# A new written-out order of instructions for block-sparse attention followed by a gated projection

## The chip, the cores and the metric

One core of one Trainium2 chip. The metric is device time in microseconds, the median of several executions. The profiled execution is one more, with its own time.

## The reference

Inputs q, k and v have 4 batches, 8 heads, 768 rows and 64 columns; `w_in` is 512 x 2048, `w_out` 2048 x 512. Every query attends to its neighbours within 15 rows and to 24 block summaries, and the result runs through two products with a hard-swish between them:

```python
k_sum = k.reshape(B, H, nb, 32, D).max(axis=3)       # nb = 24
v_sum = v.reshape(B, H, nb, 32, D).mean(axis=3)
scores_l = where(|i - j| < 16, scale * q @ k.T, -1e9)
scores_s = scale * q @ k_sum.T + log(32)
a = softmax(concat([scores_l, scores_s]))
attn = a @ concat([v, v_sum])
...
h = x @ w_in                                          # x: 3072 x 512
g = h * clip(h + 3, 0, 6) / 6
out = g @ w_out
```

## The kernel before

Attention and the two products are worked off as one stream. The 3072 tokens make eight tiles `s` = 0 to 7 of 384 (two halves for each batch); queries go in groups of 64, each with a window of 96 keys and 24 summaries, 120 keys in all. Heads go in pairs `p` = 0 to 3.

The instructions of the five engines stand in the order that the string `ORDER` gives. Every operation registers itself under a key, with what it reads, writes and which PSUM or SBUF buffers it uses. `Plan.issue` goes through the string, takes the operation with that key, gives it the buffer that has been free longest, and issues it; waits follow from the data and the buffers. An engine executes its own operations in the order of the string, so a waiting one holds up all behind it on that engine. The letter behind a colon (`:A`, `:D`) picks ACT or DVE where either can do a copy.

The keys, as far as they matter here:

- `K`, `Q`, `V`, `I`, `O`, `H`: loads, all issued by POOL. `K00` to `K02`, `Q00`, `Q01` and `V00` to `V03` bring batch 0's keys, half of its queries and its values; `Q0w0` to `Q0w2` bring the rows of its other queries in three wide chunks (tile `qwide`, lines 318 to 326; chunk 0 is two transfers, of 16 and of 112 rows); `I0`, `I2`, `I4`, `I8`, `I12` bring columns of `w_in` from 0, 256, 512, 1024 and 1536 on (line 373); `K1*` and `Q1w*` are batch 1's keys and wide queries, `O*` is `w_out`.
- `k`, `q`: transposes of keys (line 391) and queries (420) on PE, with copies. `q3` and `q2` are those of the wide chunks (441); from `q4` on those of batch 1 (439).
- `sXYZ`: scores of batch X, pair or couple Y, half Z (489, 512), the exponential on ACT, the masking on DVE. In the first half of batch 0 a product with a mask stands ahead (`cover`, 481).
- `u`: sums of values (535, 553) and their copies; `h`: copies of values' halos.
- `v0p`: values of batch 0's first half, pair p (581), with the normalisation on DVE (598, 605), a transpose on PE (589) and a copy. `v411`, `v410` and so on: the same for two pairs of later halves (623, 636).
- `F{s}x{ft}`: a group of four products with `w_in` (666), `relu` on ACT (670), `gate` on DVE (671). For tile 0 the first five column groups are issued product by product, so that pair p's share can run as soon as it is there.
- `G{s}{ts}x...`: products with `w_out` (683) in four parts, a copy, and the store on SP.
- `w`: turning batch 1's and later keys on DVE (455) and what belongs to it.
- `_n`, `-n`, `~n`, `=n`: products of a tile of ones (line 771), whose result nobody reads. `_` and `-` are n products of 64 and of 128 columns, `~` n of 512, `=` one of n times 64.

PSUM has three banks `h`, one bank `o` and two double banks `S`. Loads go round eight semaphores, so that a load is issued once the one eight earlier has landed.

Of the kernel before, what the change touches and what calls it, by code (L numbers as in the profile page):

```python
# [37 lines left out]
F0x8.1 F0x8.2 F0x5.1 I0.0 F0x5.2 F0x11.0 F0x1.0 F0x11.1 F0x11.2 F0x1.1 F0x1.2 F0x1.3 F0x1.4 F0x1.5 v410.0 v410.1 F0x7.0 F0x7.1  # L38
F0x7.2 v410.2 F0x10.0 F0x10.1 I12.0 F0x13.0 F0x13.1 F0x15.0 F0x15.1 F0x13.2 F0x10.2 v411.3 v411.4:D v410.3 v410.4:A F0x15.2
F0x14.0 F0x14.1 F0x14.2 F0x9.0 F0x9.1 F0x9.2 F0x0.0 F0x0.1 F0x2.0 F0x2.1 K13.0 K10.0 c.12:A F0x0.2 K12.0 K11.0 w10.0 Q1w1.0  # L40
F1x14.0 F1x14.1 F1x14.2 F1x4.0 F1x4.1 F1x4.2 F1x2.0 F1x2.1 F1x2.2 w10.1:D F0x2.2 F0x2.3 F0x2.4 F0x12.0 F0x12.1 F0x12.2 F1x8.0
F1x8.1 F1x8.2 F1x1.0 F1x1.1 F1x1.2 F0x0.3 F0x0.4 F0x0.5 F0x2.5 F1x9.0 F1x9.1 F1x9.2 F1x5.0 F1x5.1 F1x5.2 F1x15.0 F1x15.1 w11.0
w11.2 F1x15.2 w11.3:D Q1w4.0 Q1w2.0 Q1w0.0 w10.2 w10.3:D q6.0 q6.1:A q7.0 q7.1:A F1x7.0 F1x7.1 w11.1:A F1x7.2 F1x12.0 F1x12.1
F1x12.2 O0.0 G02x0.0 Q1w5.0 Q1w3.0 q4.0 q4.1:A q5.0 q5.1:A F1x6.0 F1x6.1 F1x6.2 O1.0 G02x0.1 s100.0 s100.1 s100.3 F1x3.0 w12.0
F1x11.0 F1x11.1 w13.0 w13.2 F1x3.1 F1x11.2 w12.2 w12.1:D O2.0 G02x0.2 s101.0 s101.1 O3.0 F1x10.0 G02x0.3 G02x0.4:A w13.3:D
w13.1:A s101.3 F1x0.0 G00x0.0 G00x0.1 w12.3:D s100.2 s101.2 s100.4 V10.0 h100.0:D F1x10.1 h110.0:A F1x10.2 F1x3.2 s110.0 s110.1
s110.2 s101.4 s110.3 G00x0.2 G00x0.3 G00x0.4:A V12.0 u4.0 h130.0:D h120.0:A F1x0.1 u4.1:D u4.2:A u4.4:D u4.3:D u4.5:D G02x0.5
G01x0.0 G01x0.1 G01x0.2 s110.4 F1x0.2 h111.0:A v100.0 v100.1 v100.2 h121.0:A v101.0 v101.1 v101.2 G01x0.3 G01x0.4:A K20.0 K21.0
K22.0 K30.0 K23.0 w21.0 F1x13.0 F1x13.1 F1x13.2 v100.3 v100.4:A w20.0 w21.3 G12x0.0 w21.2:A v101.3 v101.4:A V22.0 H2.0 h101.0:A
w20.3 G12x0.1 G12x0.2 F2x2.0 F2x2.1 F2x11.0 F2x2.2 F2x11.1 F2x11.2 s111.0 w23.0 s111.3 F2x1.0 F2x1.1 F2x1.2 F2x3.0 F2x3.1 F2x3.2  # L50
F2x15.0 F2x15.1 F2x15.2 Q22.0 w23.3 G12x0.3 s111.1 G12x0.4:A F2x5.0 F2x5.1 h131.0:A F2x5.2 F2x6.0 G10x0.0 s111.2 w22.0 w22.3
s111.4 w23.4:A V20.0 H2.1:A K33.0 F2x13.0 F2x13.1 F2x13.2 G10x0.1 F2x6.1 F2x0.0 F2x0.1 F2x0.2 u5.0 u5.1:A u5.5:A F2x6.2 v110.0
v111.0 v111.1 v111.2 Q30.0 F2x4.0 F2x4.1 F2x4.2 Q21.0 Q23.0 Q20.0 w22.4:A F2x10.0 F2x10.1 F2x10.2 F2x12.0 F2x12.1 w20.1 F2x12.2
w22.2:A v110.1 w21.4:A Q33.0 Q32.0 G10x0.2 G01x0.5 G10x0.3 G10x0.4:A v110.2 F2x8.0 F2x8.1 w21.1 w20.2:A F2x9.0 w20.4:A F2x9.1
F2x9.2 u5.2:D F2x14.0 u5.4:D w23.2:A F2x8.2 v111.3 F2x14.1 v111.4:A G11x0.0 G11x0.1 u5.3:D w22.1 v110.3 v110.4:A F2x7.0 F2x7.1
G11x0.2 F3x14.0 F3x14.1 F2x14.2 F2x7.2 F3x14.2 s200.0 s200.1 w23.1 w21.5:A s200.3 G11x0.3 F3x9.0 F3x9.1 F3x9.2 F3x8.0 F3x8.1
F3x8.2 F3x13.0 Q31.0 K31.0 s200.4 s200.2 G11x0.4:A G11x0.5 G12x0.5 s210.0 s210.3 s210.4 s210.1 s210.2 F3x4.0 F3x12.0 G22x0.0
F3x13.1 F3x13.2 H3.0 v201.0 K32.0 V32.0 w20.5:D F3x4.1 F3x4.2 V30.0 G00x0.5 F3x12.1 v200.0 v200.1 F3x2.0 v201.1 v201.2 v201.3
G22x0.1 F3x0.0 F3x0.1 G22x0.2 G22x0.3 w23.5:A G22x0.4:A F3x12.2 v200.2 v200.3 v201.5 F3x1.0 F3x1.1 F3x1.2 s201.0 w31.0 G20x0.0
v201.4 F3x0.2 F3x2.1 s201.3 F3x2.2 F3x11.0 s201.1 G20x0.1 F3x5.0 F3x11.1 F3x3.0 F3x5.1 F3x11.2 w30.0 F3x5.2 v201.7 F3x15.0  # L60
G20x0.2 F3x15.1 F3x15.2 w30.3 F3x3.1 F3x3.2 w22.5:A w30.4:D s201.4 F3x6.0 F3x6.1 H3.1:A G20x0.3 G20x0.4:A F3x7.0 F3x10.0 G21x0.0
s211.0 F3x7.1 F3x10.1 s201.2 F3x7.2 s211.3 s211.1 F3x10.2 w32.0 F3x6.2 w32.3 s211.4 s211.2 w30.2:A G21x0.1 G21x0.2 G21x0.3
G21x0.4:A u6.0 u6.1:D u6.5:A u6.4:A u6.2:A w31.3 v211.0 v201.6 v210.0 v210.1 v210.2 w31.2:D v211.1 v210.3 v211.2 v211.3 G10x0.5
w31.4:D w33.0 G32x0.0 G32x0.1 G32x0.2 G32x0.3 G32x0.4:A F4x14.0 F4x14.1 F4x14.2 F4x4.0 F4x4.1 w32.2:A F4x4.2 F4x15.0 F4x15.1
F4x15.2 w31.1 G30x0.0 G30x0.1 F4x8.0 F4x8.1 F4x8.2 F4x2.0 F4x2.1 F4x2.2 F4x13.0 G30x0.2 F4x13.1 u6.3:A F4x13.2 w33.3 F4x7.0
F4x7.1 F4x7.2 G21x0.5 G20x0.5 v211.4 F4x6.0 F4x6.1 F4x6.2 v211.7 v211.6 v211.5 w30.1 F4x11.0 F4x11.1 F4x11.2 G30x0.3 G30x0.4:A
G30x0.5 F4x1.0 F4x1.1 w33.2:A F4x1.2 w32.4:D F4x5.0 F4x5.1 F4x5.2 G22x0.5 s300.0 s300.3 s300.1 F4x3.0 F4x12.0 F4x12.1 F4x9.0
F4x3.1 F4x9.1 w31.5:A w33.4:A w33.1 w32.1 F4x9.2 F4x12.2 w32.5:D s300.2 G31x0.0 G31x0.1 G31x0.2 s300.4 F4x3.2 s310.0 s310.3
s310.4 s310.1 s310.2 F4x0.0 F4x0.1 F4x0.2 F4x10.0 G31x0.3 w30.5:A F4x10.1 w33.5:D F4x10.2 v301.0 v301.1 v300.0 v301.2 v300.1
G31x0.4:A G31x0.5 v300.2 v300.3 v301.3 F5x14.0 F5x14.1 v301.5 v301.7 v301.6 v301.4 F5x2.0 G42x0.0 G42x0.1 F5x1.0 F5x1.1 F5x2.1  # L70
G42x0.2 F5x14.2 F5x1.2 F5x2.2 s301.0 s301.3 G42x0.3 G42x0.4:D s301.1 s301.2 F5x6.0 F5x6.1 F5x6.2 F5x4.0 F5x4.1 F5x4.2 F5x3.0
s311.0 s311.3 s311.4 F5x9.0 F5x9.1 F5x9.2 F5x3.1 F5x3.2 s311.1 s311.2 s301.4 G40x0.0 F5x13.0 F5x5.0 F5x5.1 F5x0.0 G40x0.1
F5x13.1 F5x13.2 F5x5.2 F5x0.1 F5x0.2 v310.0 v311.0 F5x10.0 v310.1 v310.2 F5x7.0 F5x7.1 F5x7.2 v311.1 F5x8.0 F5x8.1 F5x8.2
# [12 lines left out]
"""


# [714 lines left out]
```

## Time and profile before

| | |
|---|---|
| three runs | 217.34, 217.96, 217.96 us; median 217.96 |
| profiled execution | 217.01 us, span 215.3 us |
| mean granted clock of TensorE | 0.998 |
| busy | PE 209.4, DVE 162.5, ACT 136.2, POOL 49.5 us |
| loads and stores | 22.68 MB, mean 105 GB/s |

Rows of a timeline read: start, length, engine, line of the kernel, operation, output<-input and size, number of instructions, and in brackets the idle time ahead of it with what ended it. PEld is the loading of weights into TensorE. Rows of the chain read: start, length, engine, output buffer, line, number. Rows of DMA issues read: output<-input, queue, number, size of each, microseconds from issue to landing.

### The profile page before, as it was taken

Reading aid. Unit: us, or ns where it says so; the run is one execution under the profiler, and the core shown is the slowest. Engines: PE = TensorE matmul, PEld = TensorE weight load, DVE = VectorE, ACT = ScalarE, POOL = GpSimd, SP = SyncE. Lnnn points to the kernel's source line nnn. Section 1 sums busy time; section 2 is a strip of 40 time slices with the busy share of each in tenths; the row PEclk is TensorE's granted clock in tenths of the full one; section 3 lists DMA queues with packets and bytes.
Section 4 is the critical chain, followed back from the end, with each engine's and each line's share of the span. In section 5 each row is a group of like instructions: output and inputs, shape, how many; then the busy total and the mean of one; then the engine's idle time right before and its main releaser. Section 6 shows DMA issues by size and latency. Waiting matters only on the chain.

```text
span 215.3 us, 6088 instructions
## 1 busy us (share of the span) xinstructions
PE 209.4 (97%) x2548; PEld 119.6 (56%) x2548; DVE 162.5 (75%) x317; ACT 136.2 (63%) x264; POOL 49.5 (23%) x66
## 2 busy tenths in 40 slices
...
GB/s 74 157 152 188 203 188 170 191 204 161 205 160 192 181 134 150 104 146 12 37 43 137 28 38 107 49 24 32 73 56 48 73 0 29 23 49 122 52 70 150
DMA packets 91580, 22.68 MB, mean 105 GB/s; under 512 B 82208, under 2 KB 88608, under 8 KB 91552
## 3 DMA queue, kind: packets, MB, share of 16 engines
...
## 4 chain that ended last, share of the span: by engine, by line
PE 86%; DMA 7%; POOL 2%; ACT 2%; DVE 1%; issue 1%; ACTq 0%; POOLq 0%
PE h L666 38%; PE o L683 33%; PE h L683 5%; DMA qwide<-in_q_dram 4%; DMA first<-in_q_dram 3%; PE S L623 3%; PE S L512 3%; PE S L553 1%; ACT vaug L241 1%; POOL first L305 1%; PE S L636 1%; PE S L439 1%; PE S L666 1%; PE h L581 1%; DVE g L671 0%
## 5 line engine op out<-in xcount | busy, mean ns | idle before, releaser
L666 PE MATMUL h<-x,win 128*128 128x384 bf16 x500 | 91.1, 326 | 0.2 <-DVE g L671 0.2
L670 ACT ACTIVATE r<-h 128x384 f32<-128x384 f32 x125 | 58.8, 492 | 38.7 <-PE h L666 36.7
L671 DVE SCALAR_TENSOR_TENSOR g<-r,h 128x384 bf16<-128x384 f32 x125 | 65.7, 546 | 22.7 <-ACT r L670 20.1
L683 PE MATMUL o<-wout,g 128*128 128x512 bf16 x336 | 81.7, 379 | 0.0
L666 PEld LDWEIGHTS <-win 128*128 128x128 bf16 x512 | 48.7, 98 | 35.8 <-issue 0.4
L683 PEld LDWEIGHTS <-g 128*128 128x128 bf16 x400 | 38.4, 98 | 37.6 <-issue 0.3
L520 ACT ACTIVATE at<-S 120x768 bf16<-120x768 f32 x24 | 18.6, 811 | 5.5 <-PE S L512 5.4
L241 ACT COPY ot<-o 128x512 f32<-128x512 f32 x17 | 10.0, 586 | 16.3 <-PE o L683 15.1
L521 DVE TENSOR_TENSOR at<-at,mask 96x768 bf16<-96x768 bf16 x24 | 12.6, 549 | 2.0 <-ACT at L520 1.6
L605 DVE TENSOR_TENSOR xn<-S,rc 128x768 bf16<-128x768 f32 x14 | 13.3, 949 | 0.3
L241 DVE COPY ot<-h 128x512 f32<-128x512 f32 x2 | 1.3, 686 | 14.1 <-PE h L683 14.1
L343 POOL DMA_DIRECT2D vaug<-in_v_dram x10 | 11.8, 1187 | 0.3 <-issue 0.2
L683 PE MATMUL h<-wout,g 128*128 128x256 bf16 (+1 forms) x64 | 11.4, 326 | 0.0
L467 DVE TENSOR_REDUCE red<-kaug 128x24 bf16<-128x768 bf16 x12 | 11.2, 941 | 0.1
L241 ACT COPY vaug<-vs 24x1536 bf16<-24x1536 bf16 x6 | 8.8, 1468 | 0.6 <-DVE vs L241 0.5
L241 ACT COPY vaug<-vaug 32x640 bf16<-32x640 bf16 (+3 forms) x17 | 8.9, 574 | 0.3 <-PE S L553 0.2
L771 PE MATMUL o<-idle 128*128 128x64 bf16 (+2 forms) x70 | 7.4, 286 | 1.1 <-DVE idle L287 1.1
L455 DVE STREAM_TRANSPOSE kaug<-kraw 128x768 bf16<-128x768 bf16 x8 | 8.1, 1020 | 0.3 <-PE S L512 0.3
L333 POOL DMA_DIRECT2D kraw<-in_k_dram x8 | 5.9, 741 | 9.1 <-DVE kaug L455 7.3
L642 DVE STREAM_TRANSPOSE y<-xn 128x768 bf16<-128x768 bf16 x8 | 7.6, 965 | 0.2
L512 PEld LDWEIGHTS <-kaug 32*128 32x128 bf16 x576 | 5.3, 92 | 4.4 <-issue 3.6
L623 PEld LDWEIGHTS <-at 120*64 120x64 bf16 x336 | 6.2, 111 | 2.6 <-issue 1.5
...
## 6 DMA issues: line engine op xcount, KB each, us to landing
out_dram<-ot SPq DMA_DIRECT2D x19, 256.0 KB, 2.3
...
first<-in_q_dram POOLq DMA_DIRECT2D x6, 192.0 KB, 12.3
```

What stands on the lines that cost most here:

```text
L241: {"ACT": nc.scalar.copy, "DVE": nc.vector.tensor_copy, "POOL": nc.gpsimd.tensor_copy}[eng](o, i)
L343: op("POOL", "dma128", lambda: nc.gpsimd.dma_start(out=o[BLK:WIN, a:z, 0:D], in_=rows[:, a:z]), w=[("v", b % 2, c) for c in range(lo, hi)] ...
L467: op("DVE", "max", lambda: nc.vector.tensor_reduce(red.slot[:], w[:, :, BLK:WIN].rearrange("p t (n c) -> p t n c", n=2), axis=AX.X, op=ALU ...
L512: nc.tensor.matmul(X[g // 2].slot[:, g % 2, i * QB:(i + 1) * QB], kaug[2 * u + m][rows, t], qT[rows, 2 * u + m, t * QB:(t + 1) * QB], star ...
L520: op("ACT", "exp", lambda a=a, e=e: nc.scalar.activation(a, X[e].slot[0:KEYS, :, 0:HALF], AF.Exp, scale=scl), r=[X[e]], w=[("at", p, half)])
L521: op("DVE", "masking", lambda m=m: nc.vector.tensor_tensor(m, m, mask[:, low(half):low(half) + HQ].unsqueeze(1).to_broadcast([WIN, 2, HQ, ...
L605: nc.vector.tensor_tensor(o, src[..., 0:D], r.unsqueeze(len(r.shape)).to_broadcast(list(o.shape)), op=ALU.mult)
L623: nc.tensor.matmul(X.slot[64 * c:64 * c + 64, i, m:m + D + 1], a[:, t * QB:(t + 1) * QB], vaug[b % 2][0:KEYS, h, t, 0:D + 1], start=True, ...
L666: nc.tensor.matmul(bank(h)[:, 0:HALF], w_in_sb[:, kt, cols], xt[s].slot[:, kt], start=(kt == 0), stop=(kt == NP - 1))
L670: op("ACT", "relu", lambda: nc.scalar.activation(r.slot[:], bank(h)[:, 0:HALF], AF.Relu, bias=0.5, scale=1.0 / 6.0), r=[h], w=[r])
L671: op("DVE", "gate", lambda: nc.vector.scalar_tensor_tensor(gt[s].slot[:, ft], r.slot[:], 1.0, bank(h)[:, 0:HALF], op0=ALU.min, op1=ALU.mul ...
L683: nc.tensor.matmul(o.slot[:, a:z], gt[s].slot[:, ft, ts * 128:(ts + 1) * 128], w_out_sb[:, ft, a:z], start=(ft == 0), stop=(ft == NFT - 1))
```

## The change

Only `ORDER` differs. It has the same 959 operations, in another order throughout; 50 copies and small steps change between ACT and DVE. The products of ones are now

```
before  _40 -15 ... ~1 =2 ... ~12 =3 ... ~2 =5 ... =1 ... ~2 =5 ... ~2 ... =1
after   _38 -17 ... =1    ... ~12 =1 ... ~2 =3 ... =1 ... =1 ... =1 ... =2
```

The core of the diff is the front, up to batch 0's last scores and the first groups:

```diff
-c.0 K00.0 c.7 c.17 c.6 c.8:A K01.0 c.10:D c.5 c.1 _40 -15 k0.0 k0.2:A c.18 ~1 =2 k1.0 K02.0 ~12 =3 k2.0 k3.0 c.15:D c.2 c.3
-s000.0 k0.3:A c.13:D c.4 c.11:A k1.1 Q00.0 q0.0 k1.4 k0.1 c.20 k1.2:A Q01.0 ~2 =5 q1.0 k0.4 k1.3:D c.9:A c.14:A c.19 k2.3:A
-q0.1:A s000.1 q0.2:A =1 s010.0 s010.1 k2.2:A k3.2:D k3.3:D k3.1 V00.0 h000.0:D h001.0:D k2.1 k2.4 s000.2 ~2 =5 v00.0 V01.0 u0.0
-h010.0:D s020.0 c.16 s010.2 q1.2:A u0.3:D u0.1:D u0.4:D v01.0 v01.1 v01.2 v00.1 q1.1:A V02.0 h020.0:A h021.0:A h011.0:A v00.2
-s020.1 v01.3 v00.3 V03.0 u1.0 u1.3:A h030.0:D s030.0 k3.4 ~2 s030.1 u1.4:D v01.4 h031.0:D Q0w0.0 Q0w1.0 v01.5:D Q0w2.0 =1 q3.0
-q3.1:D q2.0 u1.1:A u1.2:D s020.2 v02.0 v02.1 v02.2 s021.0 v02.3 s030.2 v03.0 v03.1 q2.1:A v03.2 s011.0 v03.3 v00.4 v00.5:D v02.4
-s021.1 s011.1 s021.2 v03.4 v03.5:D s011.2 v02.5:A s031.0 s031.1 s001.0 s031.2 I2.0 F0x3.0 F0x3.1 F0x3.2 F0x3.3 F0x3.4 F0x3.5
-I4.0 F0x6.0 F0x6.1 F0x6.2 F0x4.0 F0x4.1 F0x4.2 F0x4.3 v411.0 v411.1 F0x5.0 F0x4.4 F0x4.5 v411.2 s001.1 I8.0 u0.2:A s001.2 F0x8.0
...
+c.0 K00.0 c.7 c.15:A c.13:A c.6 c.14:A c.10:A c.9:D c.5 K01.0 K02.0 c.19 c.2 c.18 c.11:D c.4 c.1 c.17 _38 -17 k0.0 k0.2:A =1
+k1.0 ~12 =1 k3.0 k1.3:A k0.1 k0.4 c.3 s000.0 k1.2:D k1.1 k3.1 k1.4 c.8:A k0.3:A k2.0 k2.3:A k2.2:A Q00.0 q0.0 q0.1:D c.20 q0.2:D
+Q01.0 ~2 =3 q1.0 q1.2:D q1.1:D s000.1 =1 s010.0 s010.1 s000.2 =1 s030.0 s010.2 k3.2:A V00.0 h000.0:D v00.0 k2.1 k2.4 V01.0 u0.0
+s020.0 s020.1 h010.0:D k3.4 k3.3:A s020.2 c.16 u0.1:D u0.2:D u0.3:A u0.4:A =1 s030.1 s030.2 V02.0 h020.0:D h021.0:A V03.0 =2
+v00.1 v00.2 u1.0 v00.3 u1.1:D u1.2:D u1.3:D u1.4:A v00.4 v00.5:A v01.0 h030.0:D h001.0:D v01.1 v01.2 v01.3 Q0w1.0 Q0w2.0 Q0w0.0
+q3.0 q3.1:D q2.0 q2.1:A v02.0 v02.1 v03.0 v03.1 v02.2 v02.3 s031.0 s031.1 v03.2 v03.3 v02.4 v02.5:D I4.0 F0x4.0 v01.4 v01.5:D
+v03.4 v03.5:A h031.0:D s031.2 s021.0 s021.1 s021.2 s011.0 F0x4.1 F0x4.2 F0x4.3 I2.0 F0x3.0 F0x3.1 F0x3.2 F0x3.3 F0x4.4 F0x4.5
+F0x3.4 F0x3.5 F0x7.0 s011.1 s011.2 s001.0 F0x7.1 F0x7.2 F0x6.0 F0x6.1 F0x6.2 v411.0 v411.1 s001.1 s001.2 I8.0 F0x10.0 F0x10.1
+F0x10.2 F0x11.0 F0x11.1 F0x11.2 h011.0:A v411.2 I12.0 F0x14.0 F0x14.1 F0x5.0 F0x14.2 F0x5.1 F0x5.2 F0x15.0 F0x15.1 c.12:A v410.0
...
```

POOL's loads from the wide chunks on:

```
before  Q0w0 Q0w1 Q0w2 I2 I4 I8 I0 I12 K13 K10 K12 K11 Q1w1 Q1w4 Q1w2 Q1w0 O0 Q1w5 Q1w3 O1 O2 O3 V10 V12
after   Q0w1 Q0w2 Q0w0 I4 I2 I8 I12 Q1w4 K11 Q1w0 I0 K10 K12 K13 Q1w3 Q1w1 Q1w2 Q1w5 O0 O1 O2 O3 V12 V10
```

In its own words the change is: a new order of the front for the landings as the trace has them; late pairs' values precede the wide queries' transposes; no late products of ones.

More of the change, by code (lines that the diff above doesn't have):

```diff
@@ L38 @@
[L38 to L73, printed above, removed]
@@ new lines @@
+q3.0 q3.1:D q2.0 q2.1:A v02.0 v02.1 v03.0 v03.1 v02.2 v02.3 s031.0 s031.1 v03.2 v03.3 v02.4 v02.5:D I4.0 F0x4.0 v01.4 v01.5:D
+v03.4 v03.5:A h031.0:D s031.2 s021.0 s021.1 s021.2 s011.0 F0x4.1 F0x4.2 F0x4.3 I2.0 F0x3.0 F0x3.1 F0x3.2 F0x4.4 F0x4.5 F0x3.3
+F0x3.4 F0x3.5 F0x7.0 s011.1 s011.2 s001.0 F0x7.1 F0x7.2 F0x6.0 F0x6.1 F0x6.2 v411.0 v411.1 s001.1 s001.2 I8.0 F0x10.0 F0x10.1
+F0x10.2 F0x11.0 F0x11.1 F0x11.2 h011.0:A v411.2 I12.0 F0x14.0 F0x14.1 F0x5.0 F0x14.2 F0x5.1 F0x5.2 F0x15.0 F0x15.1 c.12:A v410.0
@@ new lines @@
+v410.1 v410.2 F0x8.0 F0x8.1 F0x15.2 F0x13.0 F0x8.2 F0x13.1 F0x13.2 v411.3 v411.4:D v410.3 Q1w4.0 K11.0 v410.4:A Q1w0.0 I0.0
+F0x1.0 F0x1.1 F0x1.2 F0x1.3 F0x1.4 F0x1.5 F0x12.0 F0x12.1 F0x12.2 F0x9.0 K10.0 F0x9.1 F0x0.0 F0x9.2 F0x2.0 K12.0 F0x0.1 F0x2.1
+F0x2.2 K13.0 w10.0 F1x5.0 F1x5.1 F1x5.2 F1x4.0 F1x4.1 F1x4.2 F0x2.3 F0x2.4 F0x0.2 F0x2.5 F0x0.3 F0x0.4 F0x0.5 F1x8.0 F1x8.1
+F1x8.2 Q1w3.0 Q1w1.0 Q1w2.0 F1x15.0 F1x15.1 F1x15.2 F1x2.0 F1x2.1 F1x2.2 w11.0 w11.2 Q1w5.0 q4.0 q4.1:A q6.0 q6.1:A F1x9.0
@@ new lines @@
+F1x9.1 F1x1.0 F1x1.1 F1x9.2 w10.2 F1x1.2 w10.3:D w11.3:D w13.0 F1x6.0 q5.0 q7.0 O0.0 G02x0.0 w11.1:A w10.1:A q7.1:A F1x7.0 O1.0
+G02x0.1 q5.1:A F1x7.1 F1x7.2 F1x6.1 F1x6.2 s100.0 s100.1 s100.3 F1x11.0 F1x14.0 F1x14.1 F1x10.0 F1x10.1 s101.0 s101.1 w13.1:D
+s101.3 O2.0 G02x0.2 w13.2 O3.0 G02x0.3 G02x0.4:A F1x14.2 F1x0.0 w12.0 w12.1:A F1x10.2 w13.3:D F1x11.1 F1x0.1 F1x3.0 G00x0.0
+w12.2 w12.3:D s110.0 s101.2 s100.4 V12.0 G00x0.1 s110.1 G00x0.2 G00x0.3 F1x0.2 F1x3.1 s100.2 s110.2 s101.4 V10.0 u4.0 h120.0:D
@@ new lines @@
+s110.3 s110.4 G00x0.4:A F1x11.2 h100.0:D u4.1:A u4.3:D u4.2:D u4.4:D u4.5:D F1x3.2 G01x0.0 G01x0.1 F1x13.0 h110.0:A v100.0
+h130.0:A h131.0:A h101.0:A v101.0 F1x13.1 G01x0.2 G01x0.3 v100.1 h111.0:A G01x0.4:A F1x12.0 F1x12.1 v101.1 v101.2 v101.3 v100.2
+v101.4:A v100.3 v100.4:A G12x0.0 G12x0.1 F2x6.0 F2x6.1 K22.0 K21.0 K20.0 K23.0 w21.0 w20.0 F1x12.2 w20.3 F1x13.2 F2x15.0 F2x6.2
+s111.0 w23.0 s111.3 w22.0 s111.1 F2x2.0 F2x2.1 Q20.0 V20.0 F2x2.2 F2x15.1 F2x15.2 F2x1.0 F2x1.1 F2x1.2 G12x0.2 s111.2 s111.4
@@ new lines @@
+w20.2:A G12x0.3 G12x0.4:A Q22.0 F2x11.0 F2x5.0 V22.0 H2.0 H2.1:D G00x0.5 w23.3 F2x12.0 F2x5.1 G10x0.0 h121.0:A w23.2:A F2x5.2
+u5.0 u5.1:A Q23.0 Q30.0 Q21.0 F2x12.1 w23.1 F2x12.2 w23.4:D w21.3 v110.0 v110.1 G02x0.5 v111.0 v111.1 v111.2 H3.0 F2x11.1
+F2x11.2 w22.2:A F2x10.0 F2x10.1 w21.2:A F2x10.2 v110.2 u5.4:A G10x0.1 G10x0.2 G10x0.3 G10x0.4:A G10x0.5 G01x0.5 F2x0.0 F2x0.1
+G12x0.5 F2x3.0 F2x14.0 F2x0.2 G11x0.0 F2x3.1 F2x3.2 w20.1 F2x14.1 w20.4:A w21.1 v111.3 v111.4:A F2x4.0 F2x4.1 F2x4.2 F2x8.0
@@ new lines @@
+F2x8.1 F2x8.2 v110.3 v110.4:A w21.4:D G11x0.1 G11x0.2 F3x0.0 u5.2:D u5.5:A F3x0.1 F3x14.0 w22.3 w22.4:D F2x14.2 F3x14.1 F3x14.2
+F3x0.2 w22.1 s200.0 s200.1 w21.5:A s200.3 s200.4 G11x0.3 G11x0.4:A F2x7.0 F3x9.0 F2x7.1 F2x7.2 F3x9.1 F3x9.2 u5.3:D F3x13.0
+F3x13.1 s210.0 s210.1 G22x0.0 s200.2 s210.2 F3x13.2 s210.3 s210.4 F2x9.0 G22x0.1 F2x9.1 F2x9.2 F2x13.0 F2x13.1 F3x11.0 F2x13.2
+v201.0 v201.1 F3x11.1 Q31.0 V30.0 K30.0 v200.0 v200.1 v200.2 F3x11.2 K33.0 V32.0 K31.0 v201.2 K32.0 v201.3 v200.3 v201.5 v201.4
@@ new lines @@
+w20.5:A F3x5.0 F3x5.1 F3x5.2 G22x0.2 G22x0.3 G22x0.4:A F3x2.0 F3x2.1 F3x6.0 F3x6.1 F3x6.2 F3x2.2 w22.5:A G20x0.0 G20x0.1 s201.0
+s201.1 w23.5:D w30.0 F3x10.0 F3x10.1 F3x10.2 F3x8.0 F3x8.1 s201.3 G22x0.5 s201.2 F3x8.2 w31.0 G20x0.2 F3x1.0 F3x1.1 F3x1.2 w31.3
+F3x7.0 F3x7.1 F3x7.2 G20x0.3 G20x0.4:A w30.2:A F3x4.0 F3x4.1 F3x4.2 s201.4 F3x3.0 G21x0.0 H3.1:A s211.0 w33.0 s211.1 s211.2
+F3x3.1 w33.3 F3x12.0 F3x15.0 F3x15.1 F3x15.2 F3x12.1 w33.2:A F3x3.2 s211.3 s211.4 G21x0.1 G21x0.2 G21x0.3 G21x0.4:A w30.3 Q33.0
```

35 lines of the change are left out of this document (23 added, 12 removed).

## The prediction

> **What bounds the kernel now.** I read the page's first part, then busy time by stretches, the chain that ended last, and the timelines of PE and POOL at the front.
>
> ```profile
> span 215.3 us, 6088 instructions
> PE 209.4 (97%) x2548; PEld 119.6 (56%) x2548; DVE 162.5 (75%) x317; ACT 136.2 (63%) x264; POOL 49.5 (23%) x66
> ```
> ```profile
> 20.00:25.00 5.00, 4.46 (x121) 3.47 (x121) 4.31 (x13) 4.07 (x6) 2.32 (x3) 1.00 1.25 206
> 40.00:45.00 5.00, 4.82 (x73) 2.84 (x71) 4.97 (x10) 4.40 (x10) 3.00 (x4) 1.00 1.43 203
> 60.00:80.00 20.00, 19.90 (x292) 11.77 (x291) 18.90 (x32) 17.77 (x35) 7.16 (x10) 1.00 1.94 171
> 200.00:215.30 15.30, 11.85 (x59) 5.59 (x57) 1.98 (x3) 1.33 (x3) 0.00 (x0) 0.97 0.29 95
> ```
>
> Behind the stretch and its length stand the busy times of PE, its weight loads, DVE, ACT and POOL, then granted clock, DMA share and GB/s. PE misses 0.54 us in 20 to 25, 0.18 in 40 to 45, 0.10 in 60 to 80 (the stretches between and behind, up to 200, miss 0.02 together). The 3.45 us missing at the end are the last copy and store. DVE, at 4.97 of 5.00, has no room in 40 to 45.
>
> ```profile
> 12.48 7.88 DMA qwide<-in_q_dram
> 20.40 0.73 PE h L441 x10
> 24.33 2.06 PE h L666 x12
> 26.39 0.50 PE S L623 x24
> 26.89 2.06 PE h L666 x12
> 28.94 0.65 PE S L666 x4
> 33.49 1.31 PE h L666 x8
> 35.62 1.96 PE h L666 x12
> 210.97 0.89 PE h L683 x8
> ```
>
> The chain has one hinge: the last chunk of the wide queries, landing at 12.48 + 7.88 = 20.36. Before it PE waits for transfers; behind it PE works without a break to 210.97 + 0.89 = 211.86. So the time is that landing, plus PE's work behind it, plus PE's idle behind it, plus 3.45 us of tail.
>
> ```profile
> 1.13 3.92 PE L771 MATMUL o<-idle 128*128 128x64 bf16 x55 [1.13 <-DVE idle L287]
> 4.98 0.85 PE L391 MATMUL h<-ident,first 96*64 96x96 bf16 x16
> 6.34 0.53 PE L391 MATMUL h<-ident,first 96*64 96x96 bf16 x16
> 12.24 0.53 PE L420 MATMUL h<-ident,first 96*64 96x96 bf16 x16 [0.22 <-DMA first<-in_q_dram]
> 13.73 0.74 PE L771 MATMUL h<-idle 128*128 128x512 bf16 x3
> 18.46 0.60 PE L771 MATMUL h<-idle 128*128 128x512 bf16 x2
> 19.27 0.35 PE L489 MATMUL S<-qT,kaug 64*128 64x64 bf16 x12 [0.21 <-DVE kaug L407]
> 19.76 0.28 PE L441 MATMUL h<-ident,qwide 128*128 128x128 bf16 x2
> 20.40 0.73 PE L441 MATMUL h<-ident,qwide 128*128 128x128 bf16 x10 [0.37 <-DMA qwide<-in_q_dram]
> 21.06 0.38 PE L581 MATMUL h<-vaug,at 96*64 96x65 bf16 x12
> 21.68 0.35 PE L489 MATMUL S<-qT,kaug 64*128 64x64 bf16 x12
> 21.96 0.38 PE L581 MATMUL h<-vaug,at 96*64 96x65 bf16 x12
> 23.53 0.34 PE L589 MATMUL h<-ident,xn 128*128 128x128 bf16 x3 [0.17 <-DVE xn L605]
> ```
>
> In this timeline the products of ones (L771) all stand ahead of 20.40; none is behind it. Of the 0.54 us, 0.37 belong to the landing, 0.17 lie behind it. PE's idle behind the hinge is thus 0.17 + 0.18 + 0.10 = 0.45 us.
>
> **Part by part.** *The ones taken out.* From 12.24 to 20.40 before has 0.74 + 0.60 us of the long ones and waits of 0.21 and 0.37; without them at most 6.3 us of work stands between the second early query group and the hinge. New PE could be through by about 18.6 (12.24 + 6.3) and would wait 1.8 us for the same landing. That wait is the cover: worth nothing while the queries land at 20.4. It also hides the early reshuffle, where pair 3's first scores go ahead of pair 0's sums: they waited for L407 at 19.27, and if that wait or one like it comes back it is short of 1.8 us. I price all of it at nothing; without that cover it would cost what it runs over 1.8 us.
>
> *Late pairs' values.* The words say that they go ahead of the wide transposes. In the lists pairs 0 and 1 were ahead already, and v02 and v03 still stand behind q3 and q2. On PE exactly the same operations lie on either side of the hinge (only xtr1 of pair 0 and of pair 1 change places). The clause moves no work: zero.
>
> *The wide chunks.* The last to land was rows 240 to 367, now it is rows 0 to 111. Before, 2 of the 12 transposes ran ahead of the landing; now the first one needs the late chunk. 2 x 0.73/10 = +0.15 us. POOL's issue is still its thirteenth, behind the same landings; its bytes fall from 128 to 112 KB, which I leave at zero.
>
> *Work behind the hinge.* The same count of every kind. A group at L666 or L683 behind small products costs more: 2.06 against 1.96 us for 12. The order returns from small products to such groups 29 times before, 30 times after: +0.10 us.
>
> *Short waits.* v02's and v03's values now run back to back, 0.62 us each (21.06 to 21.68), so the second normalised pair is wanted at about 23.3 where DVE had its second one at 23.5: a wait of 0 to 0.3, taken at 0.2. The 0.45 us of idle can go at most wholly; I take 0.3, because DVE has the same work there. The last copies change engine, PE's last two groups do not: zero, between -0.1 and +0.1.
>
> Sum on the profiled execution: 217.01 + 0.15 + 0.10 + 0.2 - 0.3 = 217.16, or +0.15 us. The median of the three runs is 217.96, 0.95 above that execution, so 218.1. Its bounds: -0.45 if all idle goes, +0.65 if the waits double and none goes: 217.5 to 218.6. About 0.65 us (0.3%) is what a measurement of this kernel can tell from no change.
>
> *What POOL's order moves.* POOL issues a load once the one eight earlier has landed, so its waits give landings.
>
> ```profile
> 13.35 0.76 POOL L373 DMA_DIRECT2D win<-in_moe_w_in_dram  x1
> 24.03 0.89 POOL L325 DMA_DIRECT2D qraw<-in_q_dram  x1 [1.42 <-DMA win<-in_moe_w_in_dram]
> 26.56 0.88 POOL L325 DMA_DIRECT2D qraw<-in_q_dram  x1 [1.64 <-DMA win<-in_moe_w_in_dram]
> 27.88 0.88 POOL L325 DMA_DIRECT2D qraw<-in_q_dram  x1 [0.44 <-DMA win<-in_moe_w_in_dram]
> 30.43 0.54 POOL L324 DMA_DIRECT2D qraw<-in_q_dram  x1 [1.67 <-DMA win<-in_moe_w_in_dram]
> 31.53 0.83 POOL L325 DMA_DIRECT2D qraw<-in_q_dram  x1 [0.56 <-DMA kraw<-in_k_dram]
> ```
> ```profile
> 36.01 1.03 DVE L455 STREAM_TRANSPOSE kaug<-kraw 128x768 bf16<-128x768 bf16 x1
> ```
>
> A wait ends 0.3 us behind the landing: win's columns 512 to 1023 landed at 23.7, 1024 to 1535 at 26.3, the first 256 at 27.6, the last 512 at 30.1; 512 KB take 2.5, 256 KB 1.3, 192 KB 1.1 us. For 128 KB I estimate 0.75 from these. All that is behind the hinge drains at one rate, so the new landings follow from the order:
>
> - Columns 512 to 1023 now precede 256 to 511: 23.7 - 1.3 = 22.4. F0x4.0 wants them behind the wide transposes, two pairs of values, scores (0.28, from 21.68 to 21.96) and one pair's transposes: 20.40 + 0.73 + 0.15 + 1.24 + 0.28 + 0.34 = 23.1.
> - Columns 1536 to 2047 no longer wait for the first 256: 28.8. F0x14 wants them behind six groups and one values2; before had done exactly that at 28.94, so about 29.1.
> - The first 256 columns go behind these and four loads: 28.8 + 0.75 + 1.1 + 0.75 + 1.3 = 32.7. F0x1 wants them behind eleven groups, which before reached at 33.49, so 33.7.
> - The raw keys of batch 1 end 3 x 1.1 later, at 36.0. DVE took the first turn at 36.01 behind 13 gates, now behind 14, a group of 0.65 later at 36.7. Behind a late turn the gates of F1x5 and F1x4 are queued, and PE's F1x15 waits for the bank that the first of them frees.
>
> The margins are 0.7, 0.3, 1.0 and 0.7 us. Before, the last columns had 2.0 (30.1 against 32.2, two groups ahead of 33.49). The new order spends most of the slack.
>
> *The rest of the lists.* Behind 45 us the orders of ACT, DVE, SP's moves and stores, and POOL's loads change too, with the same operations. Before idles 0.10 us there, so there is next to nothing to win; what a new wait costs I leave to the first rival's upper end.
>
> **The rivals.** *Landings a little late; slower.* The place is F0x14, the turn of pair 0, and the same kind of place at the wide queries of batch 1. It costs from 0.3 us late onwards, because PE has no idle to take it up and DVE is full. For it: the last query chunk itself came late by as much.
>
> ```profile
> qwide<-in_q_dram POOLq DMA_DIRECT2D x1, 128.0 KB, 7.1
> qwide<-in_q_dram POOLq DMA_DIRECT2D x1, 128.0 KB, 7.9
> q8 instruction: 1, 0.02, 5.6%
> ```
>
> Two equal loads, issued one behind the other, took 7.1 and 7.9 us, and in 18 to 19 us an instruction load shares the engines. One such 0.8 us at F0x14 costs 0.5, at the turn 0.1; three of the first kind 1.5, one alone with the forecast's own +0.15 0.65, which is where the verdict turns. Against it: the landings used here have such delays in them already. Price +1.0, between these: 219.0.
>
> *The clock falls in the 1.8 us gap; slower.* Ahead of it the products of ones kept PE busy. The grant in the last microseconds:
>
> ```profile
> 213.00:214.00 1.00, 0.00 (x0) 0.00 (x0) 0.00 (x0) 0.00 (x0) 0.00 (x0) 1.00 0.70 256
> 214.00:215.30 1.30, 0.00 (x0) 0.00 (x0) 0.00 (x0) 0.00 (x0) 0.00 (x0) 0.66 0.00 0
> ```
>
> PE stopped at 211.86 and the mean of 0.66 over 1.30 us puts a fall to half at 214.4, after 2.5 us of idleness. The new gap is shorter by 0.7 us, with thinner work ahead of it. Price: sixteen transposes took 0.85 at 4.98 and 0.53 at 6.34, so cold work costs 0.38 of its time; the ones had run from 1.13 to 6.34 at most before that, so up to 5 us, at most 1.9, and about 1.4, since part of it falls into waits: 219.4. The Trainium skill, "TensorE: Matmul & The Clock Gate", Part 1, has the clock halve after at least one idle window of about 3.4 us, by which the gap would cost nothing. Measured here it fell after 2.5 us, so I do not lean on that.
>
> *The queries land earlier; faster.* Were the instruction load to fall elsewhere, the chunk would take 7.1 and land 0.8 earlier, and PE is ready for it at 18.6. But F0x14 then meets its columns: of 0.8 only the 0.3 of margin is kept unless they too come earlier, and with all 0.45 of idle gone that makes 0.75: 217.2. Both have to happen.
>
> *The change does little of what it says.* Its second clause moves nothing on PE, its third takes out what waits anyway; that is my forecast.
>
> **How the numbers follow.** Forecast 0.40, 218.1 (own range 217.5 to 218.6). Late landings 0.35 at 219.0, clock 0.11 at 219.4, early queries 0.14 at 217.2. So faster 0.14, same 0.40, slower 0.46. The range reaches from 217.0 to 219.5 to hold 8 in 10.
>
> **What would show it.** PE idle for 1 to 2 us ahead of L441, which starts near 20.4 with 12 in a row; no PE gap over 0.3 us behind it. Wrong if L441 starts before 19.8 and the end follows, if L666 waits for win, or DVE at L455 for kraw between 28 and 41 us, if the granted clock is under 1 there, or if PE has gaps behind 45 us that I did not look for order by order.

## The result, and the profile after

The changed kernel takes 223.66 us (median of four, 223.21 to 224.12), the kernel before 217.77 us beside it (217.34 to 217.96). The ratio on record is 1.029, 95% interval 1.0269 to 1.0311 (the quotient of these two medians is 1.027): slower, and outside the range forecast. The profiled execution took 223.44 us, against 217.01 us before.

The page of the changed kernel, its first lines and the row of the granted clock in 40 slices of 5.5 us:

```profile
span 221.7 us, 6059 instructions
PE 210.7 (95%) x2517; PEld 122.8 (55%) x2544; DVE 158.5 (71%) x308; ACT 137.4 (62%) x273; POOL 49.4 (22%) x66
PEclk9998579999999999999999999999999999999999
```

PE's busy time has hardly grown (209.4 before; the trace has 2544 weight loads but 2517 matmuls, so 27 are missing), the span has grown by 6.4. The clock has a dent in the fourth to sixth slice. By stretches of 5 and 20 us (busy PE, weight loads, DVE, ACT, POOL; then clock, DMA share, GB/s):

```profile
15.00:20.00 5.00, 2.72 (x77) 2.03 (x77) 3.31 (x10) 4.49 (x10) 3.74 (x5) 1.00 2.05 173
20.00:25.00 5.00, 4.38 (x71) 3.65 (x72) 2.73 (x9) 1.99 (x5) 2.20 (x4) 0.55 1.32 203
25.00:30.00 5.00, 5.00 (x97) 3.84 (x94) 3.43 (x11) 2.75 (x4) 1.43 (x2) 0.50 1.69 186
60.00:80.00 20.00, 18.99 (x236) 10.57 (x237) 17.15 (x30) 14.72 (x30) 2.35 (x4) 1.00 1.35 121
```

PE misses 2.3 us in 15 to 20, where the prediction has a gap of 1.8; from 20 on it is busy at half the clock, which it is not in the kernel before (1.00 in 20 to 25). In 60 to 80 it misses 1.01 us, against 0.10; 0.7 of it are waits ahead of L623. PE's timeline shows the gap:

```profile
17.35 0.37 PE L581 MATMUL h<-vf,at 24*64 24x65 bf16 x12
20.62 1.46 PE L535 MATMUL o<-vaug,ind 96*32 96x128 bf16 x24 [2.90 <-ACT vaug L241]
23.39 1.46 PE L441 MATMUL S<-ident,qwide 128*128 128x128 bf16 x12
39.42 2.11 PE L666 MATMUL h<-x,win 128*128 128x384 bf16 x12
66.17 0.96 PE L623 MATMUL S<-vaug,at 120*64 120x65 bf16 x36 [0.53 <-DVE vaug L241]
```

The long wait does not stand ahead of the wide transposes (L441), which follow without one. It stands four groups earlier, ahead of the sums `u1.0` (L535), and its releaser is ACT. ACT's timeline names the copy:

```profile
16.87 0.81 ACT L495 ACTIVATE at<-S 120x768 bf16<-120x768 f32 x1 [0.43 <-PE S L489]
17.71 0.26 ACT L241 CAST vf<-h 24x128 bf16<-24x128 f32 x1
17.99 0.83 ACT L241 COPY vaug<-vf 24x768 bf16<-24x768 bf16 x1
18.83 0.81 ACT L495 ACTIVATE at<-S 120x768 bf16<-120x768 f32 x1
19.65 0.92 ACT L241 COPY vaug<-vaug 32x640 bf16<-32x640 bf16 x2
```

The last row is the halo copy `h021.0:A`, ahead of `u1.0` in the new list. The sums read rows of `vaug` in which it works, so they wait for its end at 20.57; ACT had two exponentials, a cast and a copy in front of it. In the kernel before, `h021.0` stands on ACT and ahead of the sums too, but just behind another halo copy, at 16.16. Its two copies end at 17.08, 3.5 us earlier, and the sums run at 17.35 without a wait:

```profile
16.16 0.92 ACT L241 COPY vaug<-vaug 32x640 bf16<-32x640 bf16 x2
17.35 0.85 PE L535 MATMUL o<-vaug,ind 96*32 96x128 bf16 x24
```

The twelfth group starts at 39.42 here (`F0x1`), a point in the work that the kernel before reached at 33.49. So 5.9 us are lost by then, nearly all of the 6.4.

### The profile page after: what moved, and what is told of

Read it like the earlier page. It is cut to its first block, busy times and chain, and to the rows that moved or that the text cites. A ratio compares the mean times of both kernels' runs of the same rounds, so it can differ in the third digit from the quotient of the medians.

```text
span 221.7 us, 6059 instructions
## 1 busy us (share of the span) xinstructions
PE 210.7 (95%) x2517; PEld 122.8 (55%) x2544; DVE 158.5 (71%) x308; ACT 137.4 (62%) x273; POOL 49.4 (22%) x66
## 4 chain that ended last, share of the span: by engine, by line
PE 85%; DMA 4%; SPq 3%; ACT 2%; DVE 2%; issue 1%; POOL 1%; ACTq 0%; POOLq 0%
PE h L666 37%; PE o L683 30%; PE h L683 5%; DMA first<-in_k_dram 3%; SPq L648 3%; PE S L512 2%; PE S L623 2%; DVE vaug L241 1%; PE S L489 1%; PE h L581 1%; DMA out_dram<-ot 1%; PE S L636 1%; ACT vaug L241 1%; PE S L481 1%; PE S L553 1%
## 5 line engine op out<-in xcount | busy, mean ns | idle before, releaser
L666 PE MATMUL h<-x,win 128*128 128x384 bf16 x504 | 92.5, 328 | 0.0
L683 PE MATMUL o<-wout,g 128*128 128x512 bf16 x310 | 77.1, 379 | 1.9 <-issue 0.6
L666 PEld LDWEIGHTS <-win 128*128 128x128 bf16 x512 | 49.1, 98 | 35.8 <-issue 0.7
L241 ACT COPY ot<-o 128x512 f32<-128x512 f32 x19 | 11.1, 584 | 25.9 <-PE o L683 25.7
L520 ACT ACTIVATE at<-S 120x768 bf16<-120x768 f32 x24 | 18.8, 811 | 5.2 <-PE S L512 5.1
L623 PEld LDWEIGHTS <-at 120*64 120x64 bf16 x336 | 6.3, 111 | 3.2 <-issue 1.8
L623 PE MATMUL S<-vaug,at 120*64 120x65 bf16 x336 | 7.3, 196 | 0.7 <-DVE vaug L241 0.7
L495 ACT ACTIVATE at<-S 120x768 bf16<-120x768 f32 x8 | 6.4, 809 | 2.4 <-PE S L489 2.3
L241 ACT COPY vaug<-vaug 32x640 bf16<-32x640 bf16 (+3 forms) x15 | 7.5, 554 | 0.1
L241 ACT COPY vaug<-vs 24x1536 bf16<-24x1536 bf16 x5 | 7.3, 1469 | 0.1
```

The source lines that it names most:

```text
L241: {"ACT": nc.scalar.copy, "DVE": nc.vector.tensor_copy, "POOL": nc.gpsimd.tensor_copy}[eng](o, i)
L520: op("ACT", "exp", lambda a=a, e=e: nc.scalar.activation(a, X[e].slot[0:KEYS, :, 0:HALF], AF.Exp, scale=scl), r=[X[e]], w=[("at", p, half)])
L623: nc.tensor.matmul(X.slot[64 * c:64 * c + 64, i, m:m + D + 1], a[:, t * QB:(t + 1) * QB], vaug[b % 2][0:KEYS, h, t, 0:D + 1], start=True, ...
L666: nc.tensor.matmul(bank(h)[:, 0:HALF], w_in_sb[:, kt, cols], xt[s].slot[:, kt], start=(kt == 0), stop=(kt == NP - 1))
L683: nc.tensor.matmul(o.slot[:, a:z], gt[s].slot[:, ft, ts * 128:(ts + 1) * 128], w_out_sb[:, ft, a:z], start=(ft == 0), stop=(ft == NFT - 1))
```

## The experiments

Each edit is to `ORDER`. The kernel before, run beside them, had medians of 217.33 to 217.49 us (one single execution of 427.54 stays unexplained). Each run lists its mean granted clock, and 0.008 below 1 is one stretch of 3.41 us at half clock (1.71 of 217). The mean does not count the half clock with which an execution starts, and that lasts longer in some. The profiled executions of two kernels below differ by it in the 13 products of ones near 7.5 us, first with pair 2's values ahead (mean 1.0), then with only the halo copy moved (mean 0.992):

```profile
7.43 4.20 PE L771 MATMUL o<-idle 128*128 128x512 bf16 x13
7.63 2.79 PE L771 MATMUL o<-idle 128*128 128x512 bf16 x13
```

**The halo copy behind the sums** (in the changed kernel).

```diff
-V02.0 h020.0:D h021.0:A V03.0 =2 v00.1 v00.2 u1.0 v00.3
+V02.0 h020.0:D V03.0 =2 v00.1 v00.2 u1.0 h021.0:A v00.3
```

> The halo copy of pair 2's second half goes behind the second sums of values in the list; all else as after. Theory A (the sums waited 2.9 us for that copy on ACT, and the wait let TensorE's clock fall): no PE gap over 0.5 us ahead of the sums, granted clock 0.99 or more, 217.8 to 218.6 us. Rival B (the clock falls because the products of ones are gone, at the wait for the wide queries): clock about 0.98, 220.5 us or more. Rival C (the rest of the new lists is what costs): clock 0.99 or more, but 219 to 221 us.

219.49 us (218.51 to 220.47, six runs), ratio 1.0093 [1.0059, 1.0128]. One token gives back 4.2 of the 5.9 us: the wait, with what follows from it, is shown to be the main cause. PE's timeline of this kernel:

```profile
12.67 0.53 PE L420 MATMUL h<-ident,first 96*64 96x96 bf16 x16
18.13 0.99 PE L535 MATMUL o<-vaug,ind 96*32 96x128 bf16 x24
20.94 0.83 PE L441 MATMUL S<-ident,qwide 128*128 128x128 bf16 x12 [0.56 <-DMA qwide<-in_q_dram]
62.54 0.96 PE L623 MATMUL S<-vaug,at 120*64 120x65 bf16 x36 [0.67 <-DVE vaug L241]
```

The sums run at 18.13, and the wait forecast ahead of the wide transposes appears, 0.56 us long. But the time is above the 217.8 to 218.6 expected and in the band of rival C. Two things are seen that can account for it: four of the six runs have a clock of 0.991 or 0.992, and there is a wait at 62 us. The next runs take these apart.

**Ones in the wait** (the changed kernel, its wait left as it is).

```diff
-v00.2 u1.0
+v00.2 ~13 u1.0
```

> After, with 13 products of ones of 512 columns (13 x 0.213 = 2.8 us) put into the wait ahead of the second sums; the wait for ACT stays. Theory A: the clock stays at 1.0, the sums start at 20.6 as in after, the wide transposes at about 22.3 instead of 20.4, so 217.8 + 1.9 = 219.7 us (219.2 to 220.3); the other 4 us of the loss were the clock. Rival D (the wait and what it shifts cost it all, the clock little): 222.5 to 223.7 us.

221.91 us (220.29 to 223.39, four runs), ratio 1.0215 [1.0139, 1.0292]; the one run at clock 1.0 took 220.29. The median lies between the two expectations. PE was kept busy up to the sums, and yet in the profiled execution the clock fell at 25.6, behind the small products. So the wait was not the only thing that lowers it.

**Ones in the wait and in the thin stretch**: the same `~13`, and

```diff
-v03.1 v02.2 v02.3 s031.0 s031.1 v03.2 v03.3 v02.4
+v03.1 ~2 v02.2 v02.3 s031.0 s031.1 v03.2 v03.3 ~2 v02.4
```

> As e2 (the 2.9 us wait stays, filled with ones), with 2 products of ones behind pair 3's values and 2 ahead of pair 2's transposes, so that the clock holds. It prices the wait alone. Theory A: clock 1.0, 219.2 to 220.2 us, some 2 us over before; the other 4 us of the change are the clock. Rival D: 221 us or more at full clock.

221.09 us (219.79 to 221.31, six runs), ratio 1.0168 [1.0124, 1.0212], all with the clock at 0.997 or more. So the changed kernel with its wait but the full clock takes 2.6 us less than the changed kernel, by the medians. That is less than the 4 us of theory A, and the median lies at the edge of rival D's band. Two of the six runs, at 219.79 and 219.97, fit theory A; the other four lie at 220.91 to 221.31, at the same mean clock. What parts them is not shown.

**The halo copy moved, and ones in the thin stretch**: the first edit, and

```diff
-Q0w0.0 q3.0
+Q0w0.0 ~3 q3.0
-v03.3 v02.4
+v03.3 ~2 v02.4
```

> As e1, with 3 products of ones of 512 columns in the wait for the wide queries and 2 ahead of pair 2's transposes. In six traces the clock fell behind every window of 3.41 us in which the columns that PE streamed, each weighted with the share of the array's 128 rows in use, filled 0.44 or less, and behind none with 0.50 or more. Theory R (the grant goes by such row-weighted work): the five products lift the thin windows from 0.43 to 0.6, the clock stays at 1.0, and without the fall the new lists run at 217.3 to 218.2 us. Rival B2 (it goes by PE's idle time, 0.8 us a window in e1): the first three fill the wait, the same result here; e8 parts the two. Rival C (the rest of the new lists costs too): clock 1.0, 218.5 to 219.5 us.

218.92 us (218.0 to 221.46, twelve runs), ratio 1.0066 [1.0039, 1.0093]. Ten of the twelve keep 0.997 or more; their median is 218.84, in the band of rival C: the rest of the lists costs too. Against the run above, which differs from it by the wait, its ones and the place of the others, the wait is worth 2.2 us at full clock.

**The same with ones of 32 rows** (`^`: 32 of the 128 rows of the tile, as many columns; they last as long).

```diff
-~3 q3.0 ... ~2 v02.4
+^3 q3.0 ... ^2 v02.4
```

> e5 with the five added products of ones using 32 of the array's 128 rows: the same columns, the same time on PE, a quarter of the row-weighted work (a thin window gets 0.43 + 0.04). Theory R: the clock falls in most executions, mean grant 0.99, 218.5 to 220.5 us, as e1. Rival B2 (idle time decides): clock 1.0 and the time of e5 within 0.3 us.

219.23 us (218.83 to 222.11, six runs), ratio 1.0103 [1.0052, 1.0154]. Four of six keep the clock, against ten of twelve. The number of rows makes no difference that this can tell; the theory that rows decide is not borne out.

**Late pairs' values really ahead of the wide transposes**: the first edit with pairs 2 and 3 and their normalisation ahead of `q3`; and with pair 2 alone and two products of ones.

```diff
-Q0w0.0 q3.0 q3.1:D q2.0 q2.1:A v02.0 v02.1 v03.0 v03.1 v02.2 v02.3 s031.0 s031.1 v03.2 v03.3
+Q0w0.0 v02.0 v02.1 v02.2 v03.0 v03.1 v02.3 v03.2 v03.3 q3.0 q3.1:D q2.0 q2.1:A s031.0 s031.1
```

> As e1, and the values of pairs 2 and 3 with their normalisation go ahead of the wide queries' transposes, which is what the change's words say. Theory A: 1.24 us of PE work move into the wait for the wide queries; the landing of win's last columns lets through only part of it: 0.3 to 1.2 us under e1, so 217.0 to 218.0 us. Rival: the values' own inputs come too late, and the time is that of e1 within 0.3 us.

> As e1, with pair 2's values alone ahead of the wide transposes (in e4 pair 3's came too late for that) and 2 products of ones of 512 columns between. Theory: 0.62 us of work move into the wait, 0.43 us of ones are added there; clock held in most executions; 217.0 to 217.9 us, 0.3 us under e5 at best. Rival: the clock still falls in the stretch behind, where no ones are, 218.5 to 220 us.

220.9 us (219.56 to 221.42, four runs), ratio 1.0155 [1.0107, 1.0204], and 219.77 us (219.38 to 221.34, six runs), ratio 1.0115 [1.0076, 1.0153]. Both times are above their expectations and above those of the kernels they build on (219.49 and 218.92). PE's timeline of the first:

```profile
21.43 0.38 PE L581 MATMUL o<-vaug,at 96*64 96x65 bf16 x12 [0.85 <-DVE rc L598]
22.05 1.10 PE L441 MATMUL S<-ident,qwide 128*128 128x128 bf16 x12
```

Values ahead need a bank that DVE has yet to read, so PE waits 0.85 us, and the transposes come at 22.05, later than at 20.94: these values are no filler for the landing. For the second kernel this is less sure. In its profiled execution the ones near 7.5 us took 1.4 us longer (the rows above), and the front ran later by as much.

**The kernel before without most of its late ones.**

```diff
-~1 =2 k1.0 ... ~12 =3 k2.0 ... ~2 =5 q1.0 ... ~2 =5 v00.0 ... ~2 s030.1
+=1 k1.0 ... ~12 =1 k2.0 ... ~2 =3 q1.0 ... =1 v00.0 ... =1 s030.1
```

> Before, with the late products of ones cut to about the numbers of after (1 of 512 columns fewer ahead of the second keys, two pairs fewer ahead of the first values, two fewer ahead of pair 3's scores) and no other edit. Theory A: no gap of PE gets near 2 us, the clock stays at 1.0, 217.4 to 218.2 us, no change. Rival B (the ones are what holds the clock): granted clock about 0.98, 220 us or more.

217.25 us (ten runs from 216.74, two of them at 220.17 and 221.52 with clocks of 0.974 and 0.977), beside 217.34; ratio 0.9995 [0.9974, 1.0017]. The third clause is worth nothing here while nothing else waits. It may take away some of what keeps the clock up: three of the ten runs have 0.984 or less and one 0.992, while of the 65 runs of the kernel before in these experiments five have 0.992 and none less. Where the clock falls is not shown, since the profiled execution kept it.

**The spreads at 62 us.** In all of these lists PE's values of batch 1 (L623) wait for the spreads of `u4` (`u4.2` to `u4.5`). PE's waits and DVE's timeline of the kernel with ones in the thin stretch, then DVE and ACT of the kernel before:

```profile
PE S L623 <- DVE vaug L241: 2.0, 2, 1.8
57.97 1.24 DVE L241 COPY vaug<-vaug 32x768 bf16<-32x768 bf16 x1 [1.59 <-PE S L553]
60.66 2.62 DVE L241 COPY vaug<-vs 24x1536 bf16<-24x1536 bf16 x4
```
```profile
58.92 1.82 DVE L241 COPY vaug<-vs 24x1536 bf16<-24x1536 bf16 x3
59.54 1.47 ACT L241 COPY vaug<-vs 24x1536 bf16<-24x1536 bf16 x1
61.06 0.95 PE L623 MATMUL S<-vaug,at 120*64 120x65 bf16 x48
```

Before, three spreads are on DVE, behind one halo copy and the cast, and one on ACT. The new list has all four on DVE, behind two halo copies, a masking and a gate. First this part was put into the kernel before, alone:

```diff
-u4.0 h130.0:D h120.0:A F1x0.1 u4.1:D u4.2:A u4.4:D u4.3:D u4.5:D ... s110.4 F1x0.2
+u4.0 h130.0:D h120.0:A F1x0.1 s110.4 F1x0.2 u4.1:A u4.3:D u4.2:D u4.4:D u4.5:D ...
```

> The kernel before with one thing of the changed list: batch 1's four spreads of the value sums all on DVE, behind the cast on ACT, which stands behind a halo copy there, and behind a masking and a gate. Nothing of its front is changed. Theory: the last spread ends about 1.3 us later, PE's values, which follow without a wait at 61.06 in the kernel before, wait 0.8 to 1.5 us there, and the time grows by as much: 218.1 to 218.9, ratio 1.004 to 1.007. Rival (PE makes up for it, since other products stand ready): no wait of over 0.3 us or one that goes elsewhere, 217.2 to 217.7.

218.08 us (217.72 to 218.82, twelve runs) beside 217.49; ratio 1.0034 [1.0017, 1.0051]. Waits of 0.47 and 0.32 us appear ahead of L623, as theory has it, and the time is 0.6 us longer, a little less than expected.

Then it was taken out of the changed kernel's list, at first with a mistake: the output copy `G00x0.4:A`, the masking and the gate went behind the spreads as well.

```diff
-u4.0 h120.0:D s110.3 s110.4 G00x0.4:A F1x11.2 h100.0:D u4.1:A u4.3:D u4.2:D u4.4:D u4.5:D F1x3.2 G01x0.0 G01x0.1 F1x13.0 h110.0:A
+u4.0 u4.1:D u4.2:A u4.4:D u4.3:D u4.5:D h120.0:D s110.3 h100.0:D h110.0:A s110.4 G00x0.4:A F1x11.2 F1x3.2 G01x0.0 G01x0.1 F1x13.0
```

> The kernel of the ones in the thin stretch (218.92 us median, clock 1.0 where profiled), with the spreads of batch 1's value sums handled as in the kernel before: the cast and three spreads on DVE right behind the sums, one spread on ACT, halo copies and the masking behind them. Theory (the later list's own wait): PE's values at about 62 us waited 1.76 + 0.21 us for the last spread; with it ready about 1.5 us earlier that wait is at most 0.5 us, no other of over 0.5 us comes in its place between 45 and 80, and the time falls to 217.2 to 217.9. Rival (the wait is on no path: PE would only wait later for the gates or masks that now come 0.6 to 1.1 us later): the wait at 62 us goes, PE's idle between 60 and 80 stays near 2 us, and the time stays at 218.6 to 219.2.

> The changed kernel itself with only the spreads of batch 1's value sums handled as in the kernel before; the halo copy ahead of the second sums and its wait of 2.9 us at 20.6 stay. Theory of two causes that add: the front's wait and clock (some 6 us) stay, the wait of 0.7 us at 62 goes: 222.6 to 223.3, ratio 1.021 to 1.026 to the kernel before. Rival (what comes late from the front hides behind the later list's slack, or the other way round): unchanged, 223.4 to 224.0.

224.04 us (222.74 to 226.22), ratio 1.0267 [1.0229, 1.0305], and 229.15 us (227.53 to 230.31), ratio 1.0528 [1.0487, 1.057], six runs each: 5.1 and 5.5 us slower than without the edit. It is the fault of the front once more. PE's next products with `w_out` need the bank `o` that the copy frees; in the second kernel:

```profile
66.80 2.59 PE L683 MATMUL o<-wout,g 128*128 128x512 bf16 x8 [4.09 <-ACT ot L241]
64.43:67.84 3.41, 1.04 (x5) 0.48 (x5) 2.48 (x6) 3.36 (x6) 0.00 (x0) 1.00 2.44 159
67.84:71.25 3.41, 3.41 (x32) 1.57 (x32) 0.00 (x0) 1.77 (x6) 0.00 (x0) 0.50 1.75 213
```

A wait of 4.09 us, and behind it one stretch of 3.41 us at half clock, together up to 4.09 + 1.7 = 5.8. This execution took 227.53 us, 4.1 more than the profiled one of the changed kernel, so the two do not simply add. The median's 5.5 holds runs with clocks down to 0.953, against 0.977 in the changed kernel.

The edit again, with copy, masking and gate left ahead of the spreads:

```diff
-u4.0 h120.0:D s110.3 s110.4 G00x0.4:A F1x11.2 h100.0:D u4.1:A u4.3:D u4.2:D u4.4:D u4.5:D F1x3.2
+u4.0 s110.3 s110.4 G00x0.4:A F1x11.2 u4.1:D u4.2:A u4.4:D u4.3:D u4.5:D h100.0:D h120.0:D F1x3.2
```

> The kernel of the ones in the thin stretch (218.92 us) with the cast and three spreads of batch 1's value sums on DVE right behind the sums and one spread on ACT; this time the output copy, the masking and the gate keep their places ahead of them, and two halo copies on DVE come behind. Theory (late spreads): the last spread ends near 60.2 instead of 63.3, PE's values at 62 wait at most 0.5 us in place of 1.76 + 0.21, no wait of 4 us as in the first attempt, and the time is 217.2 to 218.0. Rival (on no path): PE's idle between 60 and 80 stays near 2 us elsewhere, 218.6 to 219.2.

> The changed kernel itself with the same edit of the spreads alone. If the causes add, the wait of about 0.7 us at 65 us goes and the front's 6 us stay: 222.6 to 223.2, ratio 1.021 to 1.027. Rival (slack behind a late front): 223.4 to 224.1.

With the halo copy moved and the ones in the thin stretch: 218.16 us (217.36 to 220.44, twelve runs), ratio 1.0059 [1.0029, 1.0088], just above the 217.2 to 218.0 expected. The eight runs at 0.997 or more have a median of 217.99, against 218.84 without this edit; the other four, at 0.984 to 0.992, lie at 218.97 to 220.44. In the changed kernel alone: 223.19 us (221.65 to 224.92, six runs), ratio 1.0268 [1.0221, 1.0314], 0.5 below 223.66, in the band for parts that add, but too spread out to prove it. PE's timeline and busy time of the former:

```profile
63.37 0.82 PE L623 MATMUL S<-vaug,at 120*64 120x65 bf16 x36
64.35 0.38 PE L623 MATMUL S<-vaug,at 120*64 120x65 bf16 x12 [0.16 <-ACT vaug L241]
60.00:80.00 20.00, 19.48 (x327) 11.73 (x331) 17.95 (x32) 16.61 (x35) 1.00 (x3) 1.00 1.33 122
```

The wait of 1.8 us is gone, 0.16 is left. So the late spreads cost the changed list about 0.8 us once its front is mended, and the kernel before 0.6.

**The account.** Medians along the steps: 223.66 as changed; 221.09 with the clock held; 218.84 without the wait as well; 217.99 with the spreads in time; the kernel before 217.3 to 217.5 beside them. The clock has 2.6, the wait 2.2, the spreads 0.8. The split between clock and wait is loose: by the two faster of the six runs with the clock held, at 219.9, the clock would have 3.8 and the wait 1.0. The last 0.5 to 0.7 was not taken apart; the five added ones, which take 0.82 us (three) and 0.60 us (two) in the trace, may be part of it. Taken alone, without holding the clock, the wait has 4.2, since fewer stretches fall to half clock without it. No version was clearly faster than the kernel before.

## Why the prediction was wrong

*The step that failed* is "worth nothing while the queries land at 20.4", with "if that wait or one like it comes back it is short of 1.8 us" beside it. The cover was worked out from PE's own list: the work that stands between the second early query group and the hinge, without the waits of before. For the sums of values ahead of the hinge, I did not ask what stands ahead of their producers on ACT or DVE. The halo copy was 2.9 us late, not 0 to 1.8. The wait ate the cover, and the landing no longer was what ended last: in the changed kernel the wide transposes ran at 23.39, 2.3 us behind the chunk, as POOL's wait for it shows (a wait ends 0.3 us behind the landing):

```profile
21.44 0.83 POOL L325 DMA_DIRECT2D qraw<-in_q_dram  x1 [0.83 <-DMA qwide<-in_q_dram]
```

The cover was also mis-sized. With the halo copy moved, PE needs 7.7 us from the second early query group (L420, 12.67) to where it is ready for the wide transposes (20.94 - 0.56 = 20.38), not at most 6.3: 0.76 of it are waits for DVE, and four products of ones that the new list keeps behind that group stand in it. Of the 1.8 us 0.56 was left, and that with the chunk landing at 20.9. Nor did the landing stay at 20.4: in the changed kernel it was at 21.1, while with the ones in the thin stretch the transposes ran at 20.23, so it differs from one execution to the next.

*The rival of the clock* had the mechanism, but the gap in another place and the price too small: 1.4, at most 1.9, against 2.6 or more by the runs. I took the cold time as up to 5 us from the start of the kernel. Here it lasted three stretches of 3.41 us. Those of the changed kernel, from its trace:

```profile
17.07:20.49 3.42, 0.65 (x25) 0.51 (x19) 1.58 (x5) 3.34 (x6) 2.79 (x5) 1.00 1.73 188
20.49:23.90 3.41, 3.27 (x56) 2.74 (x56) 1.67 (x7) 0.83 (x2) 0.94 (x2) 0.50 1.32 203
23.90:27.31 3.41, 3.41 (x72) 2.85 (x71) 2.44 (x7) 1.46 (x4) 1.50 (x2) 0.50 1.32 206
27.31:30.73 3.42, 3.42 (x39) 2.21 (x38) 2.49 (x7) 2.26 (x4) 1.11 (x2) 0.50 1.94 171
30.73:34.14 3.41, 3.41 (x52) 1.99 (x51) 2.72 (x6) 2.91 (x6) 3.23 (x5) 1.00 1.76 183
```

It fell at 20.49, 2.8 us after PE's last product at 17.72; the end of the kernel before had shown 2.5. Not to lean on a whole idle window was right: the window that ended there had 0.65 us of work in it. The Trainium skill, "TensorE: Matmul & The Clock Gate", Part 1, gives the full clock back after at least one busy window; the trace differs, since the two stretches behind 20.49 were busy for 3.27 and 3.41 us and the clock stayed at half.

*The rest of the lists* I left to a rival's upper end without going through them. There was a term of 0.6 to 0.8 us in them, of the same kind as in the front: copies that stand behind other work in their engine's queue.

*What held.* The second clause moves nothing, and values moved ahead for real saved nothing (220.9 and 219.77 against 219.49). Taking out the late ones is free by itself in the kernel before, by the median. With the halo copy moved, PE does wait ahead of L441 for the chunk. No product at L666 waits for `win` in the kernels with the front's wait removed; a weight load of L666 waits once, for 0.2 us with the ones in the thin stretch and 0.3 in the first kernel with the spreads moved. So the landings that the first rival feared came just in time there. The +0.15 for the wide chunks and the margins of 0.3 to 1.0 us were too small to be seen under the rest.
